# Attention and FFN in one kernel: the PV product read a step later, casts and weight conversion regrouped beside PV, and rounding put ahead of the next absolute value

## The chip, the cores and the metric

The kernel runs on one core of a Trainium2 chip. Its engines are named as in the profile: PE multiplies matrices (PEld loads its weights), DVE is the vector engine, ACT the scalar engine, POOL is GpSimd, and SP issues all transfers here. Each engine takes its own instructions in the order in which the program wrote them for it and waits for the others by semaphores. The metric is the device time of one execution in microseconds (us). Before the change it is 770.18 us, the median of three runs (769.48 to 771.16).

## The reference, cut to what matters

```python
scores = scale * np.matmul(q, k.transpose(0, 1, 3, 2))       # 4 batches, 8 heads, 576 x 64
bias = np.maximum((psi_rel / psi_i)[..., None] @ w1 + b1, 0) @ w2
scores = scores + bias.transpose(2, 0, 1)[None]
attn = np.exp(scores - max); attn = attn / (sum + 1e-09)
x = (attn @ v) laid out as (2304 tokens, 512)
h = x @ w_in                                                  # 512 x 2048
g = np.maximum(0.01 * h, h)
out = (g @ w_out).astype(np.float32)                          # 2048 x 512
```

The two FFN weights come as 64-bit floats; everything else is 32-bit.

## The kernel before, in words

**Stages.** First the position bias is made for all heads and written to device memory (about 0 to 60 us). Then 16 attention units follow, one for each pair of heads and batch (unit 0 to 15). The FFN comes last, in blocks of 512 tokens (four of them, and one of 256); within a block it goes through 16 slices `m` of 128 hidden columns, and `seq` lists all pairs of block and slice.

**Precision by halves.** PE multiplies in a rounded 32-bit format. An operand that needs more is split into a rounded high part and the rest: a cast makes the high part, a subtraction the low part. For an attention unit DVE casts the queries (`L193`, tile `qs`) and the keys (`L198`, tile `ks`), and POOL makes the low parts, two passes for the queries (`L205`) and two for the keys (`L208`). The products are then taken with `ks1` (high) and `ks2` (low). `SPL` is the table that says at which of the nine steps of a unit each of these is written for the *next* unit.

**A unit has nine tiles** (A0, B0, A1, B1, M, A2, B2, A3, B3), and one step of the program, `step(n)` with `n = 9 u + i`, handles one tile in several phases, three steps apart. In the order of writing, a step does: the score product of tile `n` on PE (`L231`, into `ps_s`, two buffers); on DVE the bias addition and the row maximum (`L253`); on ACT the exponential (`L254`); for a finished pair of tiles the reciprocals of the row sums on DVE (`L260`, `L261`) and their spread over a tile `rb` on POOL (`L264`); where one is due, the PV product; and the transposes of tile `n - 3` on PE (`L291`, into `ps_t`, two buffers), whose results ACT copies into the tile `PT` (`L307`, `L298`) and DVE copies too (`L313`, `L301`).

**PV.** Twice in a unit, at `i = 0` and at `i = 4`, 20 matmuls multiply `PT` with the values (`L331`). Their result in `ps_o` is multiplied by the reciprocals on DVE: `L342`, and in the first block of tokens also `L338`, followed by a cast on ACT (`L339`) and a subtraction on DVE a step later (`L354`). In the kernel before, this multiplication is written in the same step as the 20 matmuls.

**Weight conversion.** A *half* is one 128 x 512 piece of `w_in` or `w_out` for a slice `m`: a 512 KB transfer into one of three buffers `raw`, then on ACT the absolute value (`L390`, into `tmp`), then on DVE four bit operations that build the 32-bit float (`L397`, `L399`, `L401`, `L403`; here b0 to b3), then the rounded copy on ACT (`L409`) and the rest on DVE (`L413`). When b3 has been written, `raw` is free, and the transfer of the third half after it is written to SP's queue. The halves of slices 0 to 4 are converted during attention (`early_ops`, 54 small pieces of work), those of slices 5 to 15 during the first FFN block from the list `todo`.

**The FFN loop.** For each slice PE runs `ffn1` (12 matmuls, `L431`) and, two slices behind, `ffn2` (12 matmuls, `L457`, `L458`, `L459`). Between them ACT makes `gh` and `g` (`L439`, `L440`), and DVE `gl` (`L446`), which `L459` reads. `work(2.6)` is called before ACT's part and again before `gl`; each call takes work from `todo` until its listed costs reach 2.6, which is five pieces on DVE, one half's worth.

Of the kernel before, what the change touches and what calls it, by code (L numbers as in the profile page):

```python
# [14 lines left out]
B, H, S, D, HID = 4, 8, 576, 64, 32  # L15
# [5 lines left out]
HS = S // 2  # L21
# [2 lines left out]
KW = 2 * S + 64  # L24
KINDS = ["A0", "B0", "A1", "B1", "M", "A2", "B2", "A3", "B3"]
GEN = [16, 17] + list(range(16)) + [34, 35] + list(range(18, 26)) + list(range(33, 25, -1))
SPL = {0: [(0, "q")], 1: [(1, "q", 0)], 2: [(0, "k")], 3: [(1, "k", 0)], 5: [(1, "q", 1)], 7: [(1, "k", 1)]}
GEN_AT = [39] * 9
LAG = 3
BLK = 512  # L30
# [5 lines left out]
def attention_ffn(ctx: ExitStack, tc: tile.TileContext, qt, kt, vm, vt, wi, wo, cst, out):  # L36
# [13 lines left out]
    def pstile(tag):  # L50
        shape = [128, 1024] if tag == "s" else [128, 512]
        return ps.tile(shape, F32, tag=tag, name="ps_" + tag)
# [163 lines left out]
    def qk_mm(n):  # L216
        u, kind = tile_id(n)
        qs, ks1, ks2 = qk[u]
        s_ = pstile("s")
        if kind == "M":  # L220
            prs = [(512, 0), (576, S + 64)]
        elif kind[0] == "A":
            prs = [(128 * int(kind[1]), 0)]
        else:
            prs = [(704 + 128 * int(kind[1]), S)]
        nmm = len(prs) * 2
        j = 0
        for c0, k0 in prs:
            for ks in (ks1, ks2):
                for hh in range(2):  # L230
                    nc.tensor.matmul(s_[:, S0 + HS * hh:S0 + HS * hh + HS], qs[:, c0:c0 + 128], ks[:, k0 + HS * hh:k0 + HS * hh + HS], start=(j == 0), stop=(j == nmm - 1))  # L231
                j += 1
        st[n] = s_
# [80 lines left out]
                if g == 1:  # L314
                    pv_q.append((at, u, 1))

    x_pend = []

    def pv():
        _, u, g = pv_q.pop(0)  # L320
        hp, b = divmod(u, B)
        if (u, g) not in pv_ps:
            pv_ps[u, g] = pstile("o")
        o, pt = pv_ps.pop((u, g)), PT.pop((u, g))
        for jb in range(5):
            for h in range(2):
                if jb < 4:
                    l, r = vv[u][:, jb, 64 * h:64 * h + 64], pt[:, 2 * jb + h, :]
                else:
                    l, r = vt_b[u % 3][:, h, :], pt[:, 8, :]  # L330
                nc.tensor.matmul(o[64 * h:64 * h + 64, 0:HS], l, r, start=(jb == 0), stop=(jb == 4))  # L331
        t0 = S * b + HS * g
        c = max(0, min(HS, BLK - t0))
        r = pt[:, 9, :]
        if c:
            x = ap.tile([128, HS], F32, tag="xt", name="xt", bufs=2)
            hi, lo = (t[:, t0:t0 + c] for t in xs[0, hp])
            nc.vector.tensor_mul(x[:, 0:c], o[:, 0:c], r[:, 0:c])  # L338
            nc.scalar.copy(out=hi, in_=x[:, 0:c])  # L339
            x_pend.append((lo, x[:, 0:c], hi))  # L340
        if c < HS:
            nc.vector.tensor_mul(x1[hp][:, t0 + c - BLK:t0 + HS - BLK], o[:, c:HS], r[:, c:HS])  # L342
# [3 lines left out]
    def step(n):  # L346
        if n < NTILE:
            qk_mm(n)
            softmax_a(n)
        if 0 <= n - 1 < NTILE and KINDS[(n - 1) % 9][0] != "A":  # L350
            recip(n - 1)
        while x_pend:
            lo, x, hi = x_pend.pop(0)
            nc.vector.tensor_sub(lo, x, hi.bitcast(F32))  # L354
        if pv_q and pv_q[0][0] <= n:
            pv()
        if 0 <= n - LAG < NTILE:
            transposes(n - LAG, n + 2)
# [110 lines left out]
    with tc.manual_schedule():  # L469
# [6 lines left out]
        early_ops = []  # L476
        for n in range(NTILE + LAG + 6):
            u, i = divmod(n, 9)
# [7 lines left out]
            if n == 8:  # L486
# [5 lines left out]
                pools["s"] = stage.enter_context(tc.tile_pool(name="stage", bufs=1, side="right"))  # L492
                pools["y"] = stage_y.enter_context(tc.tile_pool(name="stage_y", bufs=1, side="right"))
            step(n)
            if n == 13:
                w_fill()
                for m in range(5):
                    early_ops += [(w_abs, m, h) for h in range(2)]
                    early_ops += [(w_bits, m, h, k) for k in range(4) for h in range(2)]
                    if m == 0:  # L500
                        early_ops += [(w_hi, 0, h) for h in range(2)] + [(w_lo, 0, h, nc.vector) for h in range(2)]
            if n >= 20 and n % 2 and early_ops:
                f, *args = early_ops.pop(0)
                f(*args)
            if n == NTILE + 2:
                ffn1(0, 0)
            if u < HP * B:
# [4 lines left out]
                if u + 1 < HP * B:  # L512
                    for f, *args in SPL.get(i, ()):
                        (split_hi, split_lo)[f](u + 1, *args)
# [16 lines left out]
        todo = []  # L531
# [5 lines left out]
        for j, t in enumerate(halves_):  # L537
            todo += [(0.42, w_bits, *t, 0), (0.43, w_bits, *t, 1)]
            if j:
                todo.append((0.69, w_lo, *halves_[j - 1], nc.vector))  # L540
            todo += [(0.69, w_bits, *t, 2), (0.69, w_bits, *t, 3)]
            if j + 2 < len(halves_):
                todo.append((0, w_abs, *halves_[j + 2]))
            todo.append((0, w_hi, *t))
        todo.append((0.69, w_lo, *halves_[-1], nc.vector))

        def work(budget):
# [6 lines left out]
        for j in range(len(seq) + 2):  # L554
            if j < len(seq):
                n, m = seq[j]
# [57 lines left out]
```

## Time and profile before

| What | us |
|---|---|
| median of three runs | 770.18 |
| the profiled execution | 768.95 |
| its span, first to last instruction | 766.9 |
| bias stage and first unit, until the first PV | 0 to 72 |
| attention, first PV to the last PV at `i = 0` | 72 to 334.2 |
| end of attention, start of the FFN | 334.2 to 351.8 |
| first FFN block while weights are converted | 351.8 to 425.9 |
| rest of the FFN | 425.9 to 766.9 |

The profile is of one execution. A row of the timeline gives the start, the length, the engine, the line and what it writes and reads; in brackets stands how long the engine had been idle before and what ended that. A row of the chain gives the start, the length and what the end of the program waited for at that time. The mean length of an instruction includes its latency: DVE's next instruction often starts about 0.1 us before the one before it has ended, so where instructions follow each other closely the distance between two starts counts.

### The profile page before, as it was taken

How to read it: one execution, taken by the hardware profiler on the slowest of the kernel's cores; microseconds unless marked ns; L12 is line 12 of the kernel's file. 1: busy time of each engine (PE TensorE's matmuls, PEld its weight loads, DVE VectorE, ACT ScalarE, POOL GpSimd, SP SyncE). 2: the span in 40 equal slices, each digit the busy share in tenths (PEclk: the TensorE clock that was granted, in tenths of full speed). 3: DMA queues.
4: the chain of work that ended last, by engine and by line, in shares of the span. 5: the costliest groups of instructions: out<-in, count | busy, mean ns of one | idle time of the engine just before them, and what ended most of it. 6: DMA issues, size and time to landing. Idle time of an engine off the chain costs nothing.

```text
span 766.9 us, 11442 instructions
## 1 busy us (share of the span) xinstructions
PE 723.3 (94%) x4192; PEld 560.0 (73%) x4192; DVE 416.0 (54%) x1011; ACT 365.2 (48%) x797; POOL 145.3 (19%) x179
## 2 busy tenths in 40 slices
PE   6899999999899999998787999999999999999998
PEld 3237877787777787766565788888888888888897
DVE  8997888888798889748878521112211112111211
ACT  4778776776667776764444431122212222122222
POOL 2674444444334344300000000000000000000000
PEclk9999999999999999999999999999999999999999
DMA  9889736734827761102444010000100001000100
GB/s 227 257 247 274 189 92 170 173 97 137 212 59 186 198 179 52 30 1 87 137 160 134 6 56 1 0 1 1 55 1 1 0 1 56 0 1 1 55 1 28
DMA packets 30264, 68.27 MB, mean 89 GB/s; under 512 B 8192, under 2 KB 8320, under 8 KB 30208
## 3 DMA queue, kind: packets, MB, share of 16 engines
q1 hardware_dynamic: 30208, 67.54, 31.6%
q8 instruction: 33, 0.54, 0.3%
q14 instruction: 23, 0.19, 0.1%
HBM read 51.92 MB, written 15.61 MB: 88 GB/s over the span
## 4 chain that ended last, share of the span: by engine, by line
PE 65%; DVE 16%; ACT 9%; DMA 7%; issue 2%; SPq 0%; DVEq 0%; ACTq 0%
PE ps_o L431 11%; PE ps_t L431 11%; PE ps_o L331 9%; PE ps_s L458 7%; PE ps_s L457 7%; PE ps_s L459 7%; DMA raw<-wo 5%; DVE p L253 5%; PE ps_s L231 4%; ACT p L254 4%; PE ps_t L291 4%; DVE r L111 2%; DVE tmp L401 2%; ACT PT L307 2%; DVE tmp L403 1%
## 5 line engine op out<-in xcount | busy, mean ns | idle before, releaser
L446 DVE TENSOR_TENSOR gl<-g,gh 128x512 fp32r<-128x512 f32 (+1 forms) x80 | 51.0, 638 | 270.5 <-ACT g L440 270.5
L254 ACT ACTIVATE p<-p,mx 128x576 f32<-128x576 f32 x128 | 99.4, 777 | 66.1 <-DVE mx L253 42.7
L459 PE MATMUL ps_s<-woh,gl 128*128 128x512 f32 x288 | 113.6, 394 | 14.8 <-DVE gl L446 14.8
L231 PE MATMUL ps_s<-ks,qs 128*128 128x288 f32 x640 | 119.7, 313 | 2.9 <-DVE mx L253 2.9
L457 PE MATMUL ps_s<-woh,gh 128*128 128x512 f32 x288 | 113.2, 393 | 1.0 <-ACT g L440 1.0
L458 PE MATMUL ps_s<-wol,gh 128*128 128x512 f32 x288 | 113.4, 394 | 0.0
L253 DVE CUSTOM_DVE_ANT_0 p<-ps_s,bias 128x576 f32<-128x576 f32 x128 | 95.2, 753 | 14.7 <-PE ps_s L231 14.1
L231 PEld LDWEIGHTS ps_s<-ks,qs 128*128 128x128 f32 x640 | 89.6, 189 | 6.7 <-DVE mx L253 5.5
L291 PE MATMUL ps_t<-ident,p 128*128 128x128 f32 x512 | 80.2, 279 | 6.0 <-ACT PT L307 5.1
L439 ACT ACTIVATE gh<-ps_o 128x512 fp32r<-128x512 f32 (+1 forms) x39 | 21.6, 553 | 127.8 <-PE ps_o L431 127.8
L307 ACT COPY PT<-ps_t 128x512 f32<-128x512 f32 x128 | 73.2, 572 | 8.5 <-PE ps_t L291 8.0
L459 PEld LDWEIGHTS ps_s<-woh,gl 128*128 128x128 f32 x288 | 54.1, 188 | 31.4 <-DVE gl L446 19.6
L291 PEld LDWEIGHTS ps_t<-ident,p 128*128 128x128 f32 x512 | 57.7, 140 | 25.5 <-ACT PT L307 11.3
L439 ACT ACTIVATE gh<-ps_t 128x512 fp32r<-128x512 f32 (+1 forms) x39 | 21.6, 554 | 114.3 <-PE ps_t L431 114.2
L331 PE MATMUL ps_o<-PT,v 128*64 128x288 f32 x512 | 70.9, 412 | 3.0 <-ACT PT L298 3.0
L457 PEld LDWEIGHTS ps_s<-woh,gh 128*128 128x128 f32 x288 | 54.1, 188 | 13.2 <-ACT g L440 1.5
L458 PEld LDWEIGHTS ps_s<-wol,gh 128*128 128x128 f32 x288 | 54.1, 188 | 11.6
L431 PE MATMUL ps_o<-xh,wil 128*128 128x512 f32 (+1 forms) x156 | 58.4, 374 | 0.0
L431 PE MATMUL ps_t<-xh,wil 128*128 128x512 f32 (+1 forms) x156 | 58.3, 374 | 0.0
L431 PE MATMUL ps_o<-xl,wih 128*128 128x512 f32 (+1 forms) x156 | 58.2, 373 | 0.0
L431 PE MATMUL ps_t<-xl,wih 128*128 128x512 f32 (+1 forms) x156 | 58.1, 373 | 0.0
L431 PE MATMUL ps_o<-xh,wih 128*128 128x512 f32 (+1 forms) x156 | 58.0, 372 | 0.0
(93 smaller groups left out, 1148.8 us busy)
## 6 DMA issues: line engine op xcount, KB each, us to landing
raw<-kt SPq DMA_DIRECT2D x32, 304.0 KB, 6.6
scr<-e SPq DMA_DIRECT2D x32, 295.5 KB, 3.4
raw<-qt SPq DMA_DIRECT2D x32, 288.0 KB, 6.1
raw<-wi SPq DMA_DIRECT2D x16, 512.0 KB, 3.6
raw<-wo SPq DMA_DIRECT2D x16, 512.0 KB, 3.6
bias<-scr SPq DMA_DIRECT2D x16, 288.0 KB, 3.4
out<-x SPq DMA_DIRECT2D x18, 256.0 KB, 2.2
v<-vm SPq DMA_DIRECT2D x16, 256.0 KB, 5.8
```

What stands on the lines that cost most here:

```text
L231: nc.tensor.matmul(s_[:, S0 + HS * hh:S0 + HS * hh + HS], qs[:, c0:c0 + 128], ks[:, k0 + HS * hh:k0 + HS * hh + HS], start=(j == 0), stop= ...
L253: nc.vector.tensor_tensor_reduce(out=p, in0=s_[:, S0:S0 + S], in1=bt, scale=-0.125, scalar=3.4e38, op0=ALU.add, op1=ALU.min, accum_out=i)
L254: nc.scalar.activation(out=p, in_=p, func=AF.Exp, bias=i, scale=-1.0, accum_out=sm_t[n][:, col:col + 1])
L291: nc.tensor.transpose(t0[:, 128 * jb:128 * jb + 128], p[:, p0 + 128 * jb:p0 + 128 * jb + 128], ident[:])
L307: nc.scalar.copy(out=PT[u, g][:, 0:8, c].rearrange("p (j h) c -> p j h c", h=2)[:, :, h, :], in_=t0[:].rearrange("p (j c) -> p j c", j=4))
L331: nc.tensor.matmul(o[64 * h:64 * h + 64, 0:HS], l, r, start=(jb == 0), stop=(jb == 4))
L431: nc.tensor.matmul(h_[:, :N], w, x[:, :N], start=(j == 0), stop=(j == len(mms) - 1))
L439: nc.scalar.activation(out=gh[:, :N], in_=h_[:, :N], func=AF.Prelu, alpha=0.01)
L446: nc.vector.tensor_sub(gl[:, :N], g[:, :N], gh[:, :N].bitcast(F32))
L457: nc.tensor.matmul(o, gh[:, c], wt[m][2][:], start=(m == 0), stop=False)
L458: nc.tensor.matmul(o, gh[:, c], wt[m][3][:], start=False, stop=False)
L459: nc.tensor.matmul(o, gl[:, c], wt[m][2][:], start=False, stop=(m == MF - 1))
```

## The change

Four things are edited.

1. The multiplication after PV is no longer written in the step of its 20 matmuls but in the next step, after that step's `L253` and reciprocals (`pv_out`, `pv_exit`).
2. The table `SPL`: the cast of the keys goes from `i = 2` to `i = 4`, the first low pass of the keys from 3 to 5, the second low pass of the queries from 5 to 3.
3. The early conversion: not one piece at every odd `n` from 21 on, but two pieces at `i = 0` and two at `i = 4`, from `n = 18` on. The 54 pieces then end at `n = 135` (before: `n = 127`).
4. In `todo`, the rounded copy of a half is written ahead of the absolute value of the second half after it, no longer behind it.

Lines of the new kernel are 4 to 5 higher: `L390` becomes `L394`, b0 to b3 become `L401`, `L403`, `L405`, `L407`, and `L342` becomes `L344`, `L409` becomes `L413`.

```diff
-SPL = {0: [(0, "q")], 1: [(1, "q", 0)], 2: [(0, "k")], 3: [(1, "k", 0)], 5: [(1, "q", 1)], 7: [(1, "k", 1)]}
+SPL = {0: [(0, "q")], 1: [(1, "q", 0)], 3: [(1, "q", 1)], 4: [(0, "k")], 5: [(1, "k", 0)], 7: [(1, "k", 1)]}
...
     def pv():
...
-        t0 = S * b + HS * g
+        pv_out.append((hp, S * b + HS * g, o, pt[:, 9, :]))
+
+    def pv_exit():
+        hp, t0, o, r = pv_out.pop(0)
         c = max(0, min(HS, BLK - t0))
-        r = pt[:, 9, :]
...
             lo, x, hi = x_pend.pop(0)
             nc.vector.tensor_sub(lo, x, hi.bitcast(F32))
+        while pv_out:
+            pv_exit()
         if pv_q and pv_q[0][0] <= n:
             pv()
...
-            if n >= 20 and n % 2 and early_ops:
-                f, *args = early_ops.pop(0)
-                f(*args)
+            for _ in range({0: 2, 4: 2}.get(i, 0) if n >= 18 else 0):
+                if early_ops:
+                    f, *args = early_ops.pop(0)
+                    f(*args)
...
             todo += [(0.69, w_bits, *t, 2), (0.69, w_bits, *t, 3)]
+            todo.append((0, w_hi, *t))
             if j + 2 < len(halves_):
                 todo.append((0, w_abs, *halves_[j + 2]))
-            todo.append((0, w_hi, *t))
```

**DVE around PV at `i = 4` of unit 3**, before. `ks` and `raw` are the keys' high part and their loaded data, `p`, `pM` and `mx` the scores and their maximum, `x_0` the attention output; each `L253` has a second row that reads out its accumulator.

```order
L198 CAST ks_1479<-raw_79 128x1216
L253 ISA p,mx<-ps_s,bias 128x576
L253 ISA mx 128x1
L253 ISA pM,mx<-ps_s,biasM 128x576
L253 ISA mx 128x1
L260 TENSOR_SCALAR sm<-sm 128x2
L261 RECIPROCAL sm<-sm 128x2
L342 TENSOR_TENSOR x_0_69<-ps_o,PT 128x288
L399 TENSOR_SCALAR tmp<-tmp 128x512
L253 ISA p,mx<-ps_s,bias 128x576
```

The same place in the changed kernel:

```order
L253 ISA pM,mx<-ps_s,biasM 128x576
L253 ISA mx 128x1
L260 TENSOR_SCALAR sm<-sm 128x2
L261 RECIPROCAL sm<-sm 128x2
L405 SCALAR_TENSOR_TENSOR tmp<-raw,tmp 128x512 x2
L198 CAST ks_1480<-raw_79 128x1216
L253 ISA p,mx<-ps_s,bias 128x576
L253 ISA mx 128x1
L260 TENSOR_SCALAR sm<-sm 128x1
L261 RECIPROCAL sm<-sm 128x1
L344 TENSOR_TENSOR x_0_69<-ps_o,PT 128x288
```

The multiplication that reads PV's result moved behind the next `L253` and its reciprocal; two bit operations and the keys' cast stand in its place. At `i = 0` it is the same with the queries' cast.

**POOL over one unit** (spreading `rb`, low passes `qs` and `ks`, and one small copy `pM`), before:

```order
L205 TENSOR_TENSOR qs_97<-raw_80,qs_97 64x576
L264 COPY rb<-sm 128x128
L208 TENSOR_TENSOR ks_1721<-raw_81,ks_1720 128x576
L264 COPY rb<-sm 128x128 x2
L266 COPY pM<-pM 128x64
L205 TENSOR_TENSOR qs_97<-raw_80,qs_97 64x576
L264 COPY rb<-sm 128x128
L208 TENSOR_TENSOR ks_1721<-raw_81,ks_1720 128x640
```

and in the changed kernel:

```order
L205 TENSOR_TENSOR qs_97<-raw_80,qs_97 64x576
L264 COPY rb<-sm 128x128
L205 TENSOR_TENSOR qs_97<-raw_80,qs_97 64x576
L264 COPY rb<-sm 128x128 x2
L266 COPY pM<-pM 128x64
L208 TENSOR_TENSOR ks_1726<-raw_81,ks_1725 128x576
L264 COPY rb<-sm 128x128
L208 TENSOR_TENSOR ks_1726<-raw_81,ks_1725 128x640
```

The second query pass and the first key pass changed places.

**ACT in the first FFN block**, before (`wih` and `woh` are the rounded copies):

```order
L390 ACTIVATE tmp<-raw 128x512
L409 CAST woh_4504<-tmp 128x512
L390 ACTIVATE tmp<-raw 128x512
L409 CAST wih_4506<-tmp 128x512
L439 ACTIVATE gh_4536<-ps_t 128x512
L440 ACTIVATE g_4534<-ps_t 128x512
```

and in the changed kernel:

```order
L413 CAST woh_4504<-tmp 128x512
L394 ACTIVATE tmp<-raw 128x512
L413 CAST wih_4506<-tmp 128x512
L394 ACTIVATE tmp<-raw 128x512
L443 ACTIVATE gh_4536<-ps_t 128x512
L444 ACTIVATE g_4534<-ps_t 128x512
```

Each rounded copy went ahead of the absolute value that stood before it.

More of the change, by code (lines that the diff above doesn't have):

```diff
@@ L315, in transposes @@
                     pv_q.append((at, u, 1))
-    x_pend = []
+    x_pend, pv_out = [], []
     def pv():
```

## The prediction

> **What bounds the kernel now.** I read the busy times by stage first, then the chain of waits in two stages, then single rows of the timeline there. The busy times by stage (PE, PEld, DVE, ACT, POOL) for attention and for the part of the first FFN block in which weights are converted:
>
> ```profile
> 72.00:334.20 262.20, 249.62 (x1889) 199.42 (x1888) 219.79 (x623) 187.94 (x441) 106.83 (x147) 1.00 0.52 135
> 351.80:425.90 74.10, 58.77 (x241) 44.24 (x241) 59.32 (x111) 33.84 (x59) 0.00 (x0) 1.00 0.43 135
> ```
>
> In attention PE is busy for 95%, but DVE, too, for 84%. In the conversion stage nobody is full: PE and DVE both have 80%, transfers 43% of their share. A stage in which no engine is full is held by a chain. This is the chain there, one turn of it:
>
> ```profile
> 359.79 3.54 DMA raw<-wo
> 363.42 0.66 ACT tmp L390
> 364.08 0.52 ACT woh L409
> 365.23 0.68 DVE tmp L401
> 365.91 0.60 DVE gl L446
> 366.51 0.61 DVE tmp L403
> 367.19 3.76 DMA raw<-wo
> ```
>
> A transfer lands, ACT takes the absolute value of that half (`L390`), and only then the rounded copy of an *older* half (`L409`), whose data had long been there. DVE's low part waits for that copy, and behind it in DVE's queue stand b2, `gl` and b3; b3 frees the buffer for the next transfer. So each turn contains a whole landing, though three buffers exist. PE pays for it at `L459`, which reads `gl`; its waits in sum, the first and the last of them:
>
> ```profile
> PE ps_s L459 <- DVE gl L446: 14.8, 11, 1.8
> ...
> 351.78 0.50 PE L459 MATMUL ps_s<-woh,gl 128*128 128x512 f32 x1 [0.47 <-DVE gl L446]
> ...
> 425.86 0.50 PE L459 MATMUL ps_s<-woh,gl 128*128 128x512 f32 x1 [1.43 <-DVE gl L446]
> ```
>
> Eleven waits are ten turns: 425.86 - 351.78 = 74.08 us, 7.41 a turn, one slice `m` each.
>
> In attention I look at the chain from the first PV to the last at `i = 0`, with one half unit in more detail:
>
> ```profile
> 72.11 2.58 PE ps_o L331 x20
> ...
> 309.00 2.78 PE ps_o L331 x20
> ...
> 317.83 2.58 PE ps_o L331 x20
> ...
> 321.77 0.76 DVE p L253
> ...
> 322.58 0.87 ACT p L254 x2
> 323.45 0.48 ACT PT L307
> ...
> 324.63 1.06 PE ps_s L231 x8
> 325.69 2.58 PE ps_o L331 x20
> ...
> 334.16 2.65 PE ps_o L331 x20
> ```
>
> Fifteen units take 334.16 - 72.11 = 262.05 us, 17.47 each. The half from 317.83 to 325.69 belongs to unit 15, which has no early conversion and no casts: 7.86 us, a loop of PV, product, `L253`, exponential, `PT` copy, transposes, product, PV. The half before it (309.00 to 317.83, unit 14, with casts and without bit operations) takes 8.83. So a unit whose other DVE work is hidden takes 7.86 + 8.83 = 16.69, and the average one loses 0.78 on top. One cause is visible, a bit operation beside a POOL pass:
>
> ```profile
> 246.83 1.56 POOL L208 TENSOR_TENSOR ks<-raw,ks 128x640 fp32r<-128x640 f32 x1
> ...
> 247.30 1.38 DVE L399 TENSOR_SCALAR tmp<-tmp 128x512 int32<-128x512 int32 x1
> ```
>
> It takes 1.38 us instead of the 0.43 of a free one (shown below), and the next `L253` stands behind it.
>
> **The rounding ahead of the absolute value.** The copy `L409` now waits only for its own b3, so the landing leaves the chain, and what is late next is DVE's own work. Two halves and one `gl` make a turn; their distances, from a stretch in which DVE doesn't wait:
>
> ```profile
> 359.03 0.69 DVE L403 SCALAR_TENSOR_TENSOR tmp<-raw,tmp 128x512 int32<-128x512 int32 x1
> 359.63 0.42 DVE L397 TENSOR_SCALAR tmp<-tmp 128x512 f32<-128x512 f32 x1
> ...
> 360.08 0.43 DVE L399 TENSOR_SCALAR tmp<-tmp 128x512 int32<-128x512 int32 x1
> ...
> 360.43 0.69 DVE L413 TENSOR_TENSOR wil<-tmp,wih 128x512 fp32r<-128x512 f32 x1
> ...
> 361.03 0.68 DVE L401 SCALAR_TENSOR_TENSOR tmp<-raw,tmp 128x512 int32<-128x512 int32 x1
> ...
> 361.75 0.69 DVE L403 SCALAR_TENSOR_TENSOR tmp<-raw,tmp 128x512 int32<-128x512 int32 x1
> ```
>
> From b3 to b3 that is 361.75 - 359.03 = 2.72. In the other half `gl` stands between b2 and b3; by the chain above b2 to `gl` and `gl` to b3 are 0.60 each instead of 0.72 together: 3.20. A turn is 5.92 us. PE's own pace in the later, waitless part is less:
>
> ```profile
> 428.43 2.81 PE ps_o L431 x12
> ...
> 434.00 2.81 PE ps_t L431 x12
> ```
>
> 5.57 per slice. So DVE sets it: ten turns of 5.92 are 59.2 instead of 74.1, **a gain of 14.9 us**.
>
> Is the landing in time? The transfer of half `j + 2` starts at the end of b3 of half `j - 1`. With landing 3.6 and `L390` 0.66 its data are ready 4.3 us later; DVE wants them (b0) after one further b3 and one whole half, 2.72 + 3.20 = 5.92 later. 1.6 us are left, and this is the cover that hides the absolute value and the landing. On ACT, `gh` and `g` stand behind an absolute value that waits up to 1 us; `gl` is wanted 3 us after them. If landings took as long as the key transfers do under attention's load,
>
> ```profile
> raw<-kt SPq DMA_DIRECT2D x32, 304.0 KB, 6.6
> ```
>
> three buffers would allow three halves in 6.6 + 0.66 + 3.3 (b0 to b3 with `gl`) + 0.1 = 10.7 us, 7.1 a turn, and the gain would be 3. At the other end PE's pace allows 74.1 - 55.7 = 18.4. I take 14.9, since the landings of this very stage are 3.5 to 3.8 and nothing else uses the queue there.
>
> **Work moved beside PV.** Unit 15 shows DVE's free time at a PV, and the page gives the cast:
>
> ```profile
> 319.38 0.17 DVE L261 RECIPROCAL sm<-sm 128x2 f32<-128x2 f32 x1
> ...
> 320.48 0.46 DVE L342 TENSOR_TENSOR x<-ps_o,PT 128x288 f32<-128x288 f32 x1 [0.94 <-PE ps_o L331]
> 321.77 0.76 DVE L253 CUSTOM_DVE_ANT_0 p<-ps_s,bias 128x576 f32<-128x576 f32 x1 [0.84 <-PE ps_s L231]
> L198 DVE CAST ks<-raw 128x1216 fp32r<-128x1216 f32 x16 | 12.6, 785 | 0.0
> ```
>
> From about 319.5 to 321.77 DVE has nothing that it must do: 2.27 us, in which it waits twice. The multiplication leaves this place; two bit operations come, 0.8 (b1 twice) to 1.3 us (b3 twice), and a cast of 0.7 to 0.8: at most 2.1. They fit, with 0.2 us to spare, so I cost them at nothing; without PV's cover they would cost 20 pairs of about 1.1 us, 22 us. At `i = 2` the keys' cast (0.7) leaves the way of the next `L253`. No bit operation runs at the steps of POOL's second key pass any more, so the collisions (0.95 in the row above) go as well. What is left is 16.69 x 15 = 250.4 instead of 262.05, a gain of 11.7.
>
> From this I take off: the multiplication stands before the `L253` of the next tile at `i = 1` and `i = 5`, up to 0.46 us by the row above. At `i = 1` nothing waits for that tile at once; at `i = 5` ACT is nearly always still busy with the tile before, so I count 0.1 per unit, 2 us with the ends of rounding. PV's `ps_o` buffer is given back a step later, but its next writer comes three steps later, so PE doesn't wait. On SP, b3 releases transfers, and in a pair two of 512 KB now stand together; at `i = 4` of units 7 and 12 they are ahead of the loads for the unit after next. Unit 8 already waits for such a load:
>
> ```profile
> DVE qs L193 <- DMA raw<-qt: 1.7, 1, 1.7
> ```
>
> I count 1.3 more there. Two absolute values in a row on ACT (1.2 us) fall between a `PT` copy and the next exponential, where ACT waits for `L253` anyway: some tenths in five places, in the 1.3. **Gain in attention: 11.7 - 2 - 1.3 = 8.4.** Bounds: all halves like the two of unit 15 (334.16 - 325.69 = 8.47 for the second) give 245.0, a gain of 17; no pair hidden gives 250.4 + 22 = 272, a loss of 10.
>
> **The sum.** The profiled execution took 768.95 us (span 766.9). 768.95 - 14.9 - 8.4 = 745.65. The median of the runs is 1.2 above the profiled one, so I predict **746.5 us**.
>
> **The rivals.** *(a) Only the rounding pays.* The pairs delay the next `L253` about as much as the scattered pieces did, for example because POOL's second query pass, now ahead of the keys, still runs when the pair starts: a collision adds 0.95 less the spare 0.2 to a pair, and 11 of the 20 pairs eat the gain of 8.4. For it speaks the small spare time; against it that this pass starts behind `rb` of step 2 and is 1.4 long, two steps ahead of the pair. 770.2 - 14.9 = 755.3. The Trainium skill, "SBUF — State Buffer", section "Who interferes with whom", says that GpSimd and such a DVE operation take a shared port as an exclusive lock, and the later one waits for the whole of the other. The rows agree: 246.83 + 1.56 = 248.39, and the operation ended at 248.68.
>
> *(b) The chain in the FFN finds a new wait* (landings that overlap and slow each other, or `gh` behind the waiting absolute value), and a turn is 6.7: a gain of 7, and 754.5; with no gain there, 761.8. Against it: 1.6 us of slack.
>
> *(c) Both at their floors*: PE's pace and unit 15's halves, 18.4 + 17: 735; half way there, 740.
>
> *(d) Slower: the key pass is late.* POOL's first key pass now stands where the second query pass stood, behind `rb` and `pM` of step 5, and the next unit's first product needs it, whereas the query pass was needed a step later:
>
> ```profile
> 314.87 1.41 POOL L205 TENSOR_TENSOR qs<-raw,qs 64x576 fp32r<-64x576 f32 x1
> ...
> 317.07 0.76 PE L231 MATMUL ps_s<-ks,qs 128*128 128x288 f32 x4
> ```
>
> The margin is 317.07 - 316.28 = 0.79. If the pass ends later by `d`, each of 15 units loses `d` - 0.79; from `d` = 2.35 on the 23.4 us are gone. At 2.9 it is 770.2 + 15 x 2.11 - 23.4 = 778. Against it: only the cast and `rb` can hold it up, and a collision on the cast's way is 0.95, so `d` stays under 1.
>
> *(e) The moves do nothing*, since in both places a wait just as long stands behind the one removed: 770.
>
> **How the numbers follow.** Forecast 0.56, with a range of its own from 740 to 752; (a) 0.20; (b) 0.10; (c) 0.07; (d) 0.05, of which 0.01 ends near no change; (e) 0.02. The range that holds the time 8 times in 10 runs from 738 to 757: it takes in (a), the milder half of (b) and of (c). About 0.2% (1.5 us) is what a measurement of this kernel tells from no change. Faster by more: forecast, (a), (b), (c), 0.93; within: 0.03; slower: 0.04.
>
> **What would show it.** In the conversion stage: ACT's rounded copies start right behind b3, DVE's low parts no longer wait for them, and the `L459` waits of PE stand about 5.9 apart, under 0.5 us each. In attention: PVs at `i = 0` about 16.7 apart, no wait of DVE for PV's result, and bit operations at their free length (0.42 to 0.69). The forecast is wrong if turns stay above 6.4, if `L253` behind a PV starts right behind the cast instead of behind its product, or if PE waits for POOL's key pass at a unit's first product.

## The result, and the profile after

The changed kernel takes 748.69 us (median of four runs: 747.11, 747.92, 749.46, 755.12), the kernel before took 769.83 beside it. The ratio is 0.974 with a 95% interval of 0.9681 to 0.98. 746.5 was predicted, with a range of 738 to 757. The profiled execution took 747.11 us (span 745.3), 21.84 less than the profiled one of before (768.95). A run that lies far above the others of its kernel (once 1156.86 us for the kernel before, once 3905.3 for a variant, neither explained) is left out of the medians and ratios below.

The busy times in the two stages (PE, PEld, DVE, ACT, POOL, then granted clock, DMA share, GB/s), with the stretches cut at about the same events as the prediction's:

```profile
72.00:327.30 255.30, 244.45 (x1889) 193.53 (x1888) 204.54 (x623) 189.49 (x441) 111.87 (x147) 1.00 0.55 139
345.00:404.00 59.00, 57.41 (x240) 46.00 (x240) 57.97 (x110) 34.83 (x60) 0.00 (x0) 0.97 0.54 170
```

The conversion stage has about the same work in 59 us instead of 74: DVE is busy for 57.97 of 59.00 and had been for 59.32 of 74.10. No engine was full there before; now DVE is. PE is at 57.41, too, but part of that is a stretch at half clock (last section). Attention is 6.9 us shorter, and DVE has 15 us less to do in it (204.54 against 219.79): the operations are as many (623), and shorter on average.

**The conversion stage.** One stretch of its timeline, on DVE and ACT, and the first and last stop for `gl`, on PE's weight loads:

```profile
359.34 0.69 DVE L407 SCALAR_TENSOR_TENSOR tmp<-raw,tmp 128x512 int32<-128x512 int32 x1
...
360.06 0.62 ACT L413 CAST woh<-tmp 128x512 fp32r<-128x512 f32 x1 [0.56 <-DVE tmp L407]
...
360.74 0.68 DVE L417 TENSOR_TENSOR wol<-tmp,woh 128x512 fp32r<-128x512 f32 x1
...
360.98 0.68 ACT L394 ACTIVATE tmp<-raw 128x512 f32<-128x512 f32 x1 [0.30 <-DMA raw<-wo]
```

```profile
344.89 0.19 PEld L463 LDWEIGHTS ps_s<-woh,gl 128*128 128x128 f32 x1 [0.91 <-DVE gl L450]
...
404.31 0.19 PEld L463 LDWEIGHTS ps_s<-woh,gl 128*128 128x128 f32 x1 [0.40 <-DVE gl L450]
```

b3 (`L407`) ends at 360.03, the rounded copy (`L413`) starts at 360.06 and has no landing ahead of it; the absolute value (`L394`), which does wait for one, comes behind. DVE's low part (`L417`) shows no idle time before it. The ten turns take 404.31 - 344.89 = 59.42 us; before they took 74.08. The gain is 14.66.

**Attention.** The chain, PVs at the first half and at the second half of a unit: the first, those of units 8, 9 and 10 with the one that ends unit 10, and the last:

```profile
72.10 2.58 PE ps_o L331 x20
...
190.77 2.58 PE ps_o L331 x20
...
200.00 2.58 PE ps_o L331 x20
...
208.64 2.58 PE ps_o L331 x20
...
216.83 2.58 PE ps_o L331 x20
...
226.69 2.58 PE ps_o L331 x20
...
234.54 2.58 PE ps_o L331 x20
...
243.19 2.58 PE ps_o L331 x20
...
327.28 2.65 PE ps_o L331 x20
```

The fifteen units take 327.28 - 72.10 = 255.18 us instead of 262.05, a gain of 6.87. With the 14.66 that is 21.53 of the 21.84. But the units are not alike. The one from 226.69 to 243.19 takes 7.85 + 8.65 = 16.50, and so do most. The one before it (208.64 to 226.69), here called unit 9, takes 8.19 + 9.86 = 18.05, and units 1, 5 and 13 are like it. The half from 190.77 to 200.00 lasts 9.23 instead of 7.85; it is the one that waits for a load:

```profile
DVE qs L193 <- DMA raw<-qt: 4.8, 3, 2.7
...
PE ps_o L294 <- DVE PT L313: 3.2, 4, 0.8
```

These two rows are from the waits of the attention stage of the changed kernel (us in total, times, longest). The second has just four waits, one in each of the four long units. What happens there, in unit 9, on POOL and DVE:

```profile
221.72 0.37 DVE L340 TENSOR_TENSOR xt<-ps_o,PT 128x224 f32<-128x224 f32 x1
222.01 0.22 DVE L344 TENSOR_TENSOR x<-ps_o,PT 128x64 f32<-128x64 f32 x1
...
222.81 1.22 DVE L356 TENSOR_TENSOR xl<-xt,xh 128x224 fp32r<-128x224 f32 x1
223.96 0.68 DVE L313 COPY PT<-ps_o 128x512 f32<-128x512 f32 x1
```

```profile
222.37 1.42 POOL L208 TENSOR_TENSOR ks<-raw,ks 128x576 fp32r<-128x576 f32 x1
```

Units 1, 5, 9 and 13 are those in which the PVs of the first token block are finished. Its results are split at once for the FFN: a multiplication in two pieces (`L340`, `L344`), ACT's rounding (`L341`) and DVE's subtraction of it (`L356`). In the changed kernel this subtraction stands at step 6, right where POOL's first key pass (`L208`) was moved to. It takes 1.22 us and ends at 224.03, a little after POOL's pass (222.37 + 1.42 = 223.79). In the kernel before, the same subtraction in the same unit was free (0.37, at 226.08):

```profile
226.08 0.37 DVE L354 TENSOR_TENSOR xl<-xt,xh 128x224 fp32r<-128x224 f32 x1
```

The tail copy `L313` stands behind it, and PE's transposes of the `M` tile wait for `L313`.

The collision itself is not new, it has only changed its place. In the kernel before, the subtraction of the *first* PV's product of these units stood at step 1, beside POOL's first query pass, and took 1.12 to 1.38 us; in the changed kernel it takes 0.44 to 0.46. In unit 9 of before, where POOL's pass ran from 217.20 to 218.62:

```profile
217.57 1.37 DVE L354 TENSOR_TENSOR xl<-xt,xh 128x288 fp32r<-128x288 f32 x1
```

At that step it cost little: unit 1 of before, in which it took 1.12, has a first half of 79.96 - 72.11 = 7.85, as long as a clean one.

The pairs beside PV are as was hoped, in this unit too:

```profile
217.94 1.37 DVE L405 SCALAR_TENSOR_TENSOR tmp<-raw,tmp 128x512 int32<-128x512 int32 x2
219.23 0.78 DVE L198 CAST ks<-raw 128x1216 fp32r<-128x1216 f32 x1
220.77 0.76 DVE L253 CUSTOM_DVE_ANT_0 p<-ps_s,bias 128x576 f32<-128x576 f32 x1 [0.76 <-PE ps_s L231]
```

Two bit operations in 1.37 us, the cast, and then 0.76 us in which DVE still waits for the product.

### The profile page after: what moved, and what is told of

Its sections match the earlier page's. It is cut to its first block, busy times and chain, and to the rows that moved or that the text cites. A ratio compares the mean times of both kernels' runs of the same rounds, so it can differ in the third digit from the quotient of the medians.

```text
span 745.3 us, 11450 instructions
## 1 busy us (share of the span) xinstructions
PE 717.7 (96%) x4192; PEld 555.9 (75%) x4192; DVE 400.0 (54%) x1011; ACT 367.2 (49%) x797; POOL 151.3 (20%) x179
## 4 chain that ended last, share of the span: by engine, by line
PE 80%; DVE 9%; ACT 6%; DMA 3%; issue 1%; POOL 0%; DVEq 0%; POOLq 0%; ACTq 0%
PE ps_o L435 13%; PE ps_t L435 13%; PE ps_o L331 10%; PE ps_s L461 9%; PE ps_s L462 9%; PE ps_s L463 9%; PE ps_s L231 6%; PE ps_t L291 6%; DVE p L253 3%; ACT p L254 3%; DVE r L111 3%; ACT PT L307 2%; PE ps_t L122 1%; PE ps_o L122 1%; PE ps_s L122 1%
## 5 line engine op out<-in xcount | busy, mean ns | idle before, releaser
L253 DVE CUSTOM_DVE_ANT_0 p<-ps_s,bias 128x576 f32<-128x576 f32 x128 | 95.0, 752 | 29.8 <-PE ps_s L231 26.8
L443 ACT ACTIVATE gh<-ps_o 128x512 fp32r<-128x512 f32 (+1 forms) x39 | 21.5, 552 | 127.8 <-PE ps_o L435 127.8
L443 ACT ACTIVATE gh<-ps_t 128x512 fp32r<-128x512 f32 (+1 forms) x39 | 21.5, 551 | 114.4 <-PE ps_t L435 114.2
L331 PE MATMUL ps_o<-PT,v 128*64 128x288 f32 x512 | 69.2, 412 | 0.4 <-ACT PT L298 0.4
```

The lines of the kernel that those rows point to most:

```text
L253: nc.vector.tensor_tensor_reduce(out=p, in0=s_[:, S0:S0 + S], in1=bt, scale=-0.125, scalar=3.4e38, op0=ALU.add, op1=ALU.min, accum_out=i)
L443: nc.scalar.activation(out=gh[:, :N], in_=h_[:, :N], func=AF.Prelu, alpha=0.01)
```

## The experiments

Eleven variants ran, each beside runs of the kernel before. Where a change of a fraction of a per cent is judged, I use the ten turns and the fifteen units of the trace beside the whole time, because the start of the program varies: the first PV stood at 72.10 us in the changed kernel and at 74.38 in a variant that is the same up to there.

| kernel | us (median) | ratio to before, 95% | first PV to the last at a unit's first half |
|---|---|---|---|
| before | 769.83 | | 262.05 |
| changed | 748.69 | 0.974 [0.9681, 0.98] | 255.18 |
| rounding alone | 755.22 | 0.9784 [0.9762, 0.9806] | 262.13 |
| attention's edits alone | 762.87 | 0.9893 [0.9875, 0.9911] | 255.17 |
| old place of the multiplication | 758.92 | 0.9852 [0.9827, 0.9877] | see below |
| old table of casts | 748.44 | 0.9717 [0.9694, 0.974] | 255.50 |
| bit operations as before | 756.80 | 0.982 [0.9798, 0.9843] | 263.97 |
| subtraction beside PV | 745.30 | 0.966 [0.9641, 0.968] | 251.67 |
| and loads ahead of the pair | 743.66 | 0.9637 [0.9621, 0.9652] | 250.08 |
| and ACT's rounding later | 741.56 | 0.9639 [0.9617, 0.9661] | see below |

**The two halves of the change, each alone.** The rounding on the kernel before, and the changed kernel with the old rounding:

```diff
             todo += [(0.69, w_bits, *t, 2), (0.69, w_bits, *t, 3)]
+            todo.append((0, w_hi, *t))
             if j + 2 < len(halves_):
                 todo.append((0, w_abs, *halves_[j + 2]))
-            todo.append((0, w_hi, *t))
```

> The kernel before with the fourth edit alone (rounded copy ahead of the absolute value). If the two places are independent, as the sum in the prediction assumes, it takes 14.7 us off: about 755.1, ratio 0.981; the first FFN block's transfers of one kind follow each other every 5.93 us instead of 7.41. Rival: the rounding gains only because attention hands over earlier or with other buffers loaded; then it stays above 759.

> The first three edits without the fourth. Independent places: 6.9 us off, about 763, ratio 0.991, PV to PV at i = 0 16.5 us in most units and about 18 in units 1, 5, 9 and 13; the FFN block's turns stay at 7.41. Rival (attention gains nothing by itself): 768 or more.

Measured: 755.22 us (before 771.1 beside it) and 762.87. Both theories hold. The times fit two independent gains loosely: 0.9784 x 0.9893 = 0.968, where the changed kernel has 0.974 with an interval from 0.9681 on. The traces say it more closely: the time of attention is 262.13 with the rounding alone (before 262.05) and 255.17 with attention's edits alone (changed 255.18), and the ten turns of the FFN take 59.43 with the rounding alone (changed 59.42) and 75.18 with attention's edits alone (before 74.08). So neither half of the change hides or feeds the other, and rival (a), by which only the rounding pays, is excluded.

The trace of the rounding alone also shows what the changed kernel's does not. There PE has to wait for `gl` once a turn (the first such weight load of `L459`, idle time before it in brackets):

```profile
389.21 0.19 PEld L459 LDWEIGHTS ps_s<-woh,gl 128*128 128x128 f32 x1 [0.47 <-DVE gl L446]
```

Waits of about 0.5 us, one a turn, from the sixth turn on (389.21, 395.20, and so to 413.04), as predicted: DVE's pace sets the turn there. In the changed kernel's profile they are missing between the first and the last turn; the last section says why, and that it cost nothing.

**Attention's three edits, undone one at a time.** The multiplication back in PV's step:

```diff
         pv_out.append((hp, S * b + HS * g, o, pt[:, 9, :]))
+            pv_exit()
```

> The changed kernel with the multiplication after PV back in the step of its matmuls, ahead of the two bit operations and the cast. Theory (the free time beside PV is what pays): DVE then waits for PV's end first, and bit operations and cast run after it, so the next L253 comes about 1.2 to 2 us late at most PVs with pairs: 15 to 30 us slower than the changed kernel, 763 to 778. Rival: DVE catches up elsewhere in the unit (it has some 16% free), and only a few us are lost, 749 to 755.

The bit operations back at every odd step:

```diff
-            for _ in range({0: 2, 4: 2}.get(i, 0) if n >= 18 else 0):
-                if early_ops:
-                    f, *args = early_ops.pop(0)
-                    f(*args)
+            if n >= 20 and n % 2 and early_ops:
+                f, *args = early_ops.pop(0)
+                f(*args)
```

> The changed kernel with the early weight pieces back at every odd step. Theory: the scattered pieces collide with POOL's passes and stand before L253: units with pieces take 0.8 us more as before, 12 x 0.8 = 10 us, about 757 to 759. Rival: the later exit and the moved cast leave room enough, and the pieces' place matters little (748 to 751).

The casts back in their old steps:

```diff
-SPL = {0: [(0, "q")], 1: [(1, "q", 0)], 3: [(1, "q", 1)], 4: [(0, "k")], 5: [(1, "k", 0)], 7: [(1, "k", 1)]}
+SPL = {0: [(0, "q")], 1: [(1, "q", 0)], 2: [(0, "k")], 3: [(1, "k", 0)], 5: [(1, "q", 1)], 7: [(1, "k", 1)]}
```

> The changed kernel with the old table SPL: the keys' cast back at i = 2, the first key pass at 3, the second query pass at 5. Theory: the cast stands before the L253 of the third tile again, 0.7 us on DVE, and POOL's first key pass runs at the start of the pair of i = 4 and collides with it: 0.2 to 0.5 us a unit, 3 to 7 us slower, 751 to 755. Rival: the moved cast is worth nothing (within 1 us of the changed kernel).

Measured: 758.92, 756.80 and 748.44. With the old place of the multiplication the waits for PV's result are back (waits of the attention stage):

```profile
DVE x L344 <- PE ps_o L331: 24.3, 21, 1.5
...
DVE xt L340 <- PE ps_o L331: 9.2, 8, 1.3
```

33.5 us of waits in sum (15.0 in the kernel before), and behind them stand the pairs and casts: work that fills the wait in the changed kernel comes after it, in the way of `L253`. From the second PV to the last this variant takes 339.77 - 81.06 = 258.71 us; the changed kernel 327.28 - 80.28 = 247.00; and the kernel before 334.16 - 79.96 = 254.20. So bit operations and casts beside PV without the later multiplication are *worse* than the kernel before by 4.5 us; 1.9 of these are in unit 8 (20.4 against 18.4), which waits 3.6 us for its queries there, 1.7 before. The result, 758.92, lies between the theory's 763 and the rival's 755: the waits are paid, but not the whole of them.

With the bit operations as before, the time is 756.80, as the theory expected (757 to 759), and attention takes 263.97: 1.9 *more* than before. The later multiplication without the pairs leaves DVE idle beside PV and puts its work elsewhere. So these two edits gain 6.9 us together and lose 4.5 and 1.9 one without the other. But the 1.9 hold the price of the four long units, which this variant pays as well: its units 1 and 5 take 18.06 and 18.04. Without some 6.2 us for them it would stand at about 257.8, 4.3 under the kernel before (an estimate, not run). So it is not shown that the later multiplication needs the pairs in order to gain.

The casts' move is worth nothing: 255.50 against 255.18 in attention, and 748.44 against 748.69. The theory (751 to 755) falls, the rival holds.

**The four long units.** The first variant lets the subtraction `L356` run only at the steps with a PV:

```diff
-        while x_pend:
+        while x_pend and n % 9 in (0, 4):
             lo, x, hi = x_pend.pop(0)
             nc.vector.tensor_sub(lo, x, hi.bitcast(F32))
```

> The changed kernel, but the subtraction of the first token block (L356) waits until the next step with a PV (i = 0 or 4), where POOL runs no low pass. Theory: units 1, 5, 9 and 13 take 18.05 us instead of 16.5 because this subtraction now stands at i = 6 ahead of the copy L313 and runs into POOL's first key pass (1.22 instead of 0.37 us), and PE's transposes of tile M wait for that copy. Then these units come down to 16.5 to 16.8 and the kernel to about 743 (5 to 6 us off the changed kernel). Rival: the two multiplications and the cast on ACT of these units cost it, whenever the subtraction runs; then the units stay above 17.7 and the time near 748.

Measured: 745.30 us; fifteen units take 251.67, 3.5 less. PE no longer waits for `L313` at `L294`. The four units take 17.1 us instead of 18.05, not the 16.5 to 16.8 that was expected: between theory and rival, so some 0.95 of the 1.55 us came from the subtraction's place and 0.6 from something else. The chain in unit 9 of this variant shows the rest:

```profile
209.38 2.58 PE ps_o L331 x20
...
214.99 0.21 ACT xh L341
...
217.56 2.58 PE ps_o L331 x20
...
222.54 0.29 DVE xt L340
...
222.83 0.13 DVE x L344
```

The first half is 8.18 long, against 7.85 in a clean unit; ACT's rounding `L341` stands in it, ahead of the `PT` copy. In the second half the two multiplications stand ahead of `L253`, in the chain.

The second variant also moves the loads for the unit after next ahead of the pair that releases two transfers:

```diff
+            if i == 4 and u + 2 < HP * B:
+                load_unit(u + 2)
             for _ in range({0: 2, 4: 2}.get(i, 0) if n >= 18 else 0):
```

(and takes them away where they stood, some lines below).

> As sub_beside_pv, and at i = 4 the loads of the unit after next are written to SP's queue ahead of the two early weight pieces. Theory: unit 8 takes 17.87 instead of 16.5 us because two weight transfers of 512 KB stand ahead of its successor's queries; with the order turned its wait for the queries (2.7 us) shrinks by some 2 us and the unit to about 16.6: 1.2 us less than sub_beside_pv, about 742. Rival: transfers are limited by the rate of the bias and query loads of this unit anyway; then no difference (under 0.4 us).

Measured: 743.66, 1.64 less, as expected. The wait for queries, before (subtraction beside PV) and after this edit:

```profile
DVE qs L193 <- DMA raw<-qt: 4.6, 3, 3.0
```

```profile
DVE qs L193 <- DMA raw<-qt: 0.8, 1, 0.8
```

The third takes ACT's rounding out of the multiplication's place and issues it behind the step's transposes, so behind the `PT` copy:

```diff
-            nc.scalar.copy(out=hi, in_=x[:, 0:c])
-            x_pend.append((lo, x[:, 0:c], hi))
+            x_cast.append((lo, x[:, 0:c], hi))
...
             transposes(n - LAG, n + 2)
+        while x_cast:
+            lo, x, hi = x_cast.pop(0)
+            nc.scalar.copy(out=hi, in_=x)
+            x_pend.append((lo, x, hi))
```

> ScalarE's rounding of the first block's product (L341) leaves the multiplication's place and is issued behind the step's transposes, so behind the PT copy; the rest is as in sub_and_load. Theory: the 0.33 us by which the first half of the four units 1, 5, 9 and 13 was still longer there (8.18 against 7.85) was that rounding, 0.21 us long, ahead of the PT copy: those halves come to 7.9, four times 0.3 less, about 1.2 us, so 742.4 where sub_and_load had 743.66. Rival: the extra is the second multiplication on VectorE ahead of L253, and the halves stay at 8.18: 743.7, no difference.

Measured: 741.56 beside a kernel before of 769.66, ratio 0.9639. Its chain:

```profile
83.25 2.58 PE ps_o L331 x20
...
208.12 2.58 PE ps_o L331 x20
...
215.97 2.58 PE ps_o L331 x20
...
324.16 2.65 PE ps_o L331 x20
```

The first half of unit 9 is now 215.97 - 208.12 = 7.85, so the cause was ACT's rounding. The four units take 16.75 to 16.83 here; the 0.3 us over a clean unit that is left in each stays unexplained. From the second PV to the last it is 240.91 us; the variant before had 323.50 - 81.60 = 241.90. That is the gain of about 1 in attention; the ratios to before (0.9639 and 0.9637) cannot show it, and whether the whole kernel gains stays open. Both variants compute everything and beat the changed kernel by about 5 us or more.

**What sets the turn of the FFN now.** Three variants of the one with the earlier loads. The first leaves a DVE operation away, the clamp of the absolute value:

> As sub_and_load, but in the first FFN block the clamp of the absolute value (the first of the four bit operations of a half, 0.46 us) is left out of the conversion of the later weight blocks; nothing else moves. Theory: VectorE's work alone sets the turn (5.93 us after the change, without a gap), so two clamps less would make it 5.1, and TensorE's own pace of 5.57 decides: ten turns of 5.57, 3.6 us less, about 740. TensorE then never waits for L450. Rival: the turn of 5.93 is set by something else that VectorE only follows (the chain of one half through ScalarE's rounding, or the weight's arrival): turns stay near 5.9 and the time near 743.7.

Measured: 742.09 (ratio 0.9635, the variant it is made from 0.9637): no difference. The theory falls as it stood: `gl` starts every 5.89 us on DVE, not every 5.1. DVE has gaps now, twice a turn:

```profile
362.47 0.69 DVE L417 TENSOR_TENSOR wol<-tmp,woh 128x512 fp32r<-128x512 f32 x1 [0.35 <-ACT woh L413]
...
365.66 0.69 DVE L417 TENSOR_TENSOR wil<-tmp,wih 128x512 fp32r<-128x512 f32 x1 [0.35 <-ACT wih L413]
```

The clamp was the cover: between b3 and the low part of the same half stood two short operations, 0.8 us, and ACT's rounding needs about as long. Take one away, and the next one in the queue waits instead. So I moved the low part one operation later, with the clamp still left out:

```diff
-            if j:
-                todo.append((0.69, w_lo, *halves_[j - 1], nc.vector))
-            todo += [(0.69, w_bits, *t, 2), (0.69, w_bits, *t, 3)]
+            todo.append((0.69, w_bits, *t, 2))
+            if j:
+                todo.append((0.69, w_lo, *halves_[j - 1], nc.vector))
+            todo.append((0.69, w_bits, *t, 3))
```

> As ffn_no_clamp (the first bit operation of a half left out in the first FFN block), and the low-part subtraction of the half before (L417) issued behind the third bit operation instead of ahead of it. In ffn_no_clamp VectorE stood 0.35 us, twice a turn, ahead of L417 for ScalarE's rounding L413, and the turn was 5.89. Theory: VectorE's work is 5.93 less two clamps, about 5.1, and with L417 one operation of 0.6 us later the rounding is there in time; TensorE's 5.57 decides, ten turns give 3.2 us less than ffn_no_clamp, about 739 where that had 742. Rival: a turn has another limit near 5.9 (the raw weights' arrival, or ScalarE's chain for a half): 742, turns of 5.9.

Measured: 740.00 (ratio 0.9601 [0.9573, 0.963]), 2.1 less than without this move; 3.2 less were expected. On DVE the theory's step shows: `gl` starts every 5.1 to 5.5 us, the raw weights of one kind are requested as often, and after the first turn PE waits for `gl` no more. But the 2.1 us are not seen in these turns. PE's weight loads at their start and end, in the variant without the clamp and in this one:

```profile
340.85 0.19 PEld L463 LDWEIGHTS ps_s<-woh,gl 128*128 128x128 f32 x1 [0.44 <-DVE gl L450]
...
399.90 0.19 PEld L463 LDWEIGHTS ps_s<-woh,gl 128*128 128x128 f32 x1
```

```profile
338.57 0.19 PEld L463 LDWEIGHTS ps_s<-woh,gl 128*128 128x128 f32 x1 [0.45 <-DVE gl L450]
...
397.62 0.19 PEld L463 LDWEIGHTS ps_s<-woh,gl 128*128 128x128 f32 x1
```

Ten turns take 59.05 us in both. That is PE's own time: ten slices of 5.57, a stop of 1.6 for `g` in the first turn and 1.7 for a stretch of half clock (last section), 59.0. It hides what DVE gained. The two profiled executions differ by 2.24 us (743.07 and 740.83), and their first PVs already by 73.46 - 71.21 = 2.25, with the same instructions up to there. So whether this move gains time is not shown; what it does to DVE's queue is. The 5.93 of the changed kernel are DVE's queue: its work *and* the distance that this work keeps between b3 and the low part.

The third gives one of the two low parts of each turn to the idle GpSimd:

```diff
-                todo.append((0.69, w_lo, *halves_[j - 1], nc.vector))
+                todo.append((0.69, w_lo, *halves_[j - 1], nc.gpsimd if j % 2 else nc.vector))
```

> As sub_and_load, but one of the two low-part subtractions of each turn of the first FFN block (L417 of after, 0.68 us on VectorE) goes to GpSimd, which is idle there. Theory by counting VectorE's work: 5.93 - 0.6 = 5.33, under TensorE's 5.57: 3.6 us less, about 740. Rival, by the rows of unit 9 (VectorE's subtraction over two SBUF operands took 1.22 instead of 0.44 us beside GpSimd's 1.42-us subtraction of 576 columns): GpSimd's subtraction of 512 columns, some 1.3 us, stretches a VectorE operation beside it by 0.7 to 1.0 us, more than the 0.6 it saves; turns of 6.0 to 6.3 and 744.5 to 747.

Measured: 748.89 (three runs, 747.45 to 750.35), ratio 0.9727 against 0.9637: slower than its base by 5 us or more. The rival holds, with a larger price than expected: a turn is 6.5 instead of 6.0 to 6.3. (The 0.44 that it names is the time of 288 columns; the 224 of the row at 1.22 take 0.37 alone.)

```profile
361.39 1.29 POOL L417 TENSOR_TENSOR wil<-tmp,wih 128x512 fp32r<-128x512 f32 x1 [5.21 <-ACT wih L413]
```

```profile
361.49 1.74 DVE L405 SCALAR_TENSOR_TENSOR tmp<-raw,tmp 128x512 int32<-128x512 int32 x1
```

DVE's `L405` begins 0.10 us behind POOL's subtraction and takes 1.74 us where it takes 0.69 alone. POOL ends at 362.68, DVE at 363.23, as if it had got nothing done until POOL had ended and then needed 0.55. By the Trainium skill, "SBUF — State Buffer", section "Who interferes with whom", a DVE operation with two SBUF inputs and a GpSimd operation that reads SBUF exclude each other for the whole instruction. This row agrees, and so does `L356` in unit 9 (ended 0.24 after POOL's pass). Had the two only shared the bandwidth, POOL's time would have grown as well; but by the 1.42 of its pass over 576 columns, 512 should take 1.26 (an estimate), and it took 1.29.

## Why the prediction was right, and where it was not

**The rounding: right, in mechanism and size.** 14.9 us were predicted and 14.66 measured; a turn was to be 5.92 and is 59.42 / 10 = 5.94. The landing left the chain, the copy follows b3 in 0.03 us, and DVE's own queue is late next. The bounds of 3 and 18.4 were not needed, and rival (b) (turns of 6.7) is out. One sentence was too simple: "DVE sets it" by its work. The run without the clamp shows that two operations fewer hardly make the turn shorter (5.89), since the wait for ACT's rounding, which these two hide, comes in their place.

**Work beside PV: right.** The pairs were costed at nothing, with "0.2 us to spare" behind pair and cast. There were 0.76 in unit 9. The bit operations are near their free lengths: in the changed kernel, and before, in the groups of the attention stage (mean ns of one behind the busy time):

```profile
L405 DVE SCALAR_TENSOR_TENSOR tmp<-raw,tmp 128x512 int32<-128x512 int32 x10 | 6.8, 729 | 0.0
```

```profile
L401 DVE SCALAR_TENSOR_TENSOR tmp<-raw,tmp 128x512 int32<-128x512 int32 x10 | 9.3, 932 | 0.0
```

(`L405` of the changed kernel is `L401` of before, b2.) The base, 16.69 a unit, was slightly high: clean units take 16.50, 0.19 x 15 = 2.9 us better over all.

**The step that failed: "so I count 0.1 per unit, 2 us", the price of the later multiplication.** The place was right (ahead of `L253` at steps 1 and 5), the distribution and the size were not. Eleven units pay nothing that can be seen (16.50 is under the base without it), and four pay 1.55 each, 6.2 in all. What was overlooked is that the multiplication isn't alone: in the units of the first token block ACT's rounding and DVE's subtraction are tied to it and moved with it, and the subtraction met POOL's key pass at its new place. The prediction knew both halves of this, the collision of a DVE operation with a POOL pass and that the first key pass moved to step 5, but had looked for the collision only at the bit operations and, in rival (a), at the query pass. The trace of before had this collision at this very line, too (`L354`, 1.37 us at 217.57), at a step where it cost little. The experiment with the subtraction beside PV gives back 3.5 of these 6.2 us, ACT's rounding behind the `PT` copy about 1 more.

**The loads at unit 8: the size is right in part by luck.** 1.3 us were taken off; the half takes 9.23 instead of a clean half's 7.85, 1.38 more, and moving the loads ahead of the pair gave 1.6 back. But the 1.3 were meant on top of the wait of 1.7 that was there before, and the base of 16.69 holds no such wait. The wait grew by 1.0, to 2.7, and about half of the 2.7 makes the unit longer than a clean one.

**The casts' move: a step that did nothing.** That the keys' cast "leaves the way of the next `L253`" at step 2 was counted as part of the 11.7. Undone, it changes attention by 0.3 us. What attention gained comes from the other two edits together.

**The sum.** Predicted 14.9 + 8.4 = 23.3, found 14.66 + 6.87 = 21.5. In attention 11.7 - 2 - 1.3 was predicted. By what was measured it is: 17.47 - 16.50 in fifteen units, 14.6, less 6.2 for the four long units, less 1.4 at unit 8, 7.0. The two errors, 2.9 too little and 4.2 too much, cancelled in part, which is luck: the time is nearer to the forecast than its terms are.

**Rival (d)** had a real mechanism (POOL's key pass, moved late) at the wrong victim: in the changed kernel no first product of a unit waits for the key pass. The pass delays a DVE operation beside it instead, and at 1.55 in four units this is far from the 23 us that it would have needed. Rival (c) needed PE's pace in the FFN and halves like unit 15's, 7.86 and 8.47; the clean halves are 7.85 and 8.65, and the FFN stays at DVE's pace. Rival (e), no change, is out by 21 us.

## What to carry to other kernels

An operation that is moved takes its followers on other engines along: list every instruction that is issued behind it (here a rounding and a subtraction in four of sixteen units) and look at each one's new neighbours, not only at the moved one's. Two moves that look like separate gains can be one exchange: filling a wait and moving the waiting operation away from it gained 6.9 us together, and filling it without moving the operation lost 4.5. And before work is taken from an engine that shows no gap, ask which of its operations stands between a value that is sent away and its return: without it, a gap opens that is nearly as long (0.35 us here, for an operation of 0.42). And a gain of two us in the whole time is not yet one in the stage that was changed: the stage's own rows have to show it.

## What the runs showed of the hardware that was not expected

In the changed kernel PE waits for `gl` at the first and the last turn only, though DVE's turn (5.93) is longer than PE's (5.57). The reason is a stretch of half clock (5-us rows, and single 1-us slices of the granted clock: 1.00 at 346, 0.50 from 348 to 351, 1.00 from 352 on):

```profile
345.00:350.00 5.00, 3.41 (x10) 2.41 (x11) 4.90 (x10) 3.47 (x6) 0.00 (x0) 0.79 0.43 133
350.00:355.00 5.00, 5.00 (x21) 4.00 (x20) 4.90 (x11) 2.79 (x5) 0.00 (x0) 0.87 0.55 185
```

Matmuls follow each other in 0.43 us there instead of 0.23. It lasts about 3.4 us and puts PE 1.7 behind; DVE runs on at its pace and PE makes up 5.93 - 5.57 = 0.36 us a turn. In the kernel with the rounding alone, without such a stretch, PE has caught up at the sixth turn; 1.7 / 0.36, some five turns, later is the end of the stage. In the changed kernel it cost nothing: the ten turns take 59.42 us with it and 413.04 - 353.61 = 59.43 without it, in that kernel:

```profile
353.61 0.19 PEld L459 LDWEIGHTS ps_s<-woh,gl 128*128 128x128 f32 x1 [0.91 <-DVE gl L446]
...
413.04 0.19 PEld L459 LDWEIGHTS ps_s<-woh,gl 128*128 128x128 f32 x1 [0.51 <-DVE gl L446]
```

With a quicker DVE queue it does cost: in the two variants without the clamp, which have such a stretch as well, the ten turns are PE's 59.05 us, and 1.7 of these are the stretch.

In the changed kernel the stretch follows this stop, whose idle time is 1.59 us, with a shorter one (0.48) 2.8 us ahead of it:

```profile
347.69 0.66 PE L461 MATMUL ps_s<-woh,gh 128*128 128x512 f32 x1 [1.59 <-ACT g L444]
```

The Trainium skill, "TensorE: Matmul & The Clock Gate", section "Part 1: The HAM clock gate", says that PE falls to half clock after an idle window of about 3.4 us, comes back after a busy one of the same length, and that the windows run freely. The length of the stretch agrees, but no wait here is that long: 3.4 us that are mostly idle seem to be enough, if they fall into one window. That the same two stops in the rounding alone (0.47 and 1.6 us) are followed by no slow stretch fits a window that runs freely; which window it was is not shown by any row, so this cause is argued, not shown. Stretches of half clock also stand in the program's first stage, where one execution had one of about 3.4 us and another, of the same instructions up to there, had twice that length (the granted clock is the third number from the end):

```profile
20.00:30.00 10.00, 8.98 (x54) 2.05 (x55) 8.77 (x19) 8.71 (x21) 6.87 (x4) 0.83 0.85 252
```

```profile
20.00:30.00 10.00, 8.20 (x50) 2.16 (x50) 7.51 (x16) 9.72 (x22) 4.84 (x3) 0.66 0.82 252
```

The first row is the changed kernel's, the second that of the rounding alone, whose first PV came at 73.85 instead of 72.10. The stretches are not the whole of it: the first PV stands at 71.21 in the timeline of the variant with the later low part, which has no stretch there, and at 75.33 in that with ACT's rounding later, which has one. So between executions the start alone moves the time by up to 4.1 us, which is more than some of the effects measured here.
